# Weighted low powers by exponentials instead of doubling products, modulation rows between the first products, a sine ahead of the arc tangent, one block's seeds three slots earlier

## The chip, the cores and the metric

The kernel runs on one core of a Trainium2 chip. The metric is the device time of one execution in microseconds. The engines are TensorE (PE, with its weight loads PEld), VectorE (DVE), ScalarE (ACT), GpSimd (POOL) and SyncE (SP), which here only issues DMAs. Each engine takes its instructions in program order, and engines wait for each other by semaphores.

## The reference

A layer norm with modulation, a long convolution with a state-space kernel, a residual, a second modulated layer norm, and a bilinear gated unit with a residual. L = 2048 tokens, D = 640 channels, N = 192 states per channel, F = 1536.

```python
sa, ca, ga, sb, cb, gb = (silu(c) @ w_mod).reshape(6, D)
h = layernorm(x) * (1 + ca) + sa
K[d, l] = Re sum_n C[d,n] * exp(dt[d] * A[d,n] * l) * dt[d] * B[d,n]      # l = 0..2047
x = x + ga * (causal_conv(h, K) + h * Dskip)                             # by FFT of length 2 L
h = layernorm(x) * (1 + cb) + sb
x = x + gb * (((h @ w_gate) * (h @ w_up)) @ w_down)
```

## The kernel before

**What is computed where.** The channels are cut into five blocks of 128 (`db`), each into two halves of 64 (`hf`), each half into four groups of 16 channels (`n`, 40 in all). For a group the long kernel K is the product of two small tables over the states: `Pt` holds 32 coarse powers and `Qt` 64 fine powers of each state, each as magnitude times cosine and magnitude times sine. PE multiplies them (`kg`, `kg_ma` and `kg_mb`), ACT copies the result out (`Kt`), and PE runs a four-step FFT of it, the product with the FFT of the input, and the way back (`u_k`, `u_pre`, `u_g`, `u_c`, `u_d`). The FFT work of a block goes on between the tables of later blocks.

**How a group's tables come about.** POOL makes the phases as 32-bit integers (`Ph`, outer sum of low phases `LH` and high phases `DH`), the magnitudes of the coarse table (`EP`, outer product of `LP` and `RH`) and of the fine table (`EQ`, outer product of `LQ` and `RH`): `outer`, L817. ACT takes absolute value, sine and cosine of the phases into a two-buffer ring in PSUM (`tra`, `trb`, function `trig`, three calls a group: `kg_aq`, `kg_ap`, `kg_b`). DVE multiplies them with the magnitudes (`QtA`, `PtA`, `PtB`, `QtB`). `Ph`, `EQ` and `EP` have two buffers each; the `QtA`, `PtB`, `QtB` tiles have one.

**Seeds.** For each block `u_seeds` prepares the state parameters: log radius and frequency (transposed by PE into the layout of the groups), the amplitude `amp` of C times B, and its angle by an arc tangent. Its steps carry letters; `SEG0` (first block) and `SEG` (others) say which steps run in one stretch. Step `r` multiplies the log radii by constants (`RL`, `RH`), step `e` takes exponentials (`LP`, `RH`, `RL`), step `f` makes the argument of the arc tangent, `g` the arc tangent, `h` its transpose, `v` the phase seed `psi`. Each function set of ACT has to be loaded before its functions run: ACT_TABLE_LOAD.

**Low tables.** Once a half, POOL makes `LH` (function `tab_ph`, by additions that double the length) and `LQ` (function `tab_eq`: a copy of the amplitude and three products that double the length: the eight weighted fine powers 0 to 7). Two small POOL operations a half (L752, L753, lambda `weighted`) first put `psi` into the low phases.

**Modulation.** `u_modr` multiplies silu(c) with the columns of `w_mod` for the six modulation rows, on PE in two pieces a row (L458); ACT copies a row out, PE transposes it (`u_fold`, L477), DVE makes the fold `mcol` from them (L481 to L491), which later seeds (`need(1, "gg")`) and the convolution input (`need(1, "sh")`) need. For the first block the gate `ga` is applied by POOL to the convolution's input (L966). `u_stats` takes the layer norm's sums of each of 16 token rows on DVE (L568, L569), `row_stats` makes their scales.

**What sets the order.** A table of numbers, `SCHED`. The program counts slots: group n has three, t = 3n, 3n+1, 3n+2; the number v // 1000 is 2t or 2t+1 and the rest orders the pieces within it. Negative numbers lie in the first block's seeds. Pieces are issued in exactly this order on every engine. A second table, `SLOT`, says which buffer of a ring each use takes. `LATE` holds the exponentials of the second half of the first block, run at slot 15 (`e0`).

After the last group (slot 240) only FFT work remains, then the gated unit, a chain of `fp32r` matrix products on PE with its operands split in high and low parts on ACT, DVE and POOL.

## Time and profile before

| | |
|---|---|
| three runs | 990.01, 992.87, 998.23 us (median 992.87) |
| the profiled execution | 990.33 us, span of its instructions 988.6 us |
| busy in the span | PE 90%, PEld 73%, DVE 77%, ACT 59%, POOL 58% |
| stages by the trace | start and first groups 0 to 100 us; tables and FFT to about 435 us (POOL's last table ends at 435 us); FFT alone to about 490 us; gated unit to the end |

The page gives busy time of each engine, the chain of work that ended last, and groups of equal instructions with busy time, mean duration, and the engine's idle time before them with its releaser. The chain is followed back from the last instruction; an engine that is busy all the time need not be on it. Matmuls are pipelined, so a busy PE is not PE at its peak.

### The profile page before, as it was taken

Reading aid. Unit: us, or ns where it says so; the run is one execution under the profiler, and the core shown is the slowest. Engines: PE = TensorE matmul, PEld = TensorE weight load, DVE = VectorE, ACT = ScalarE, POOL = GpSimd, SP = SyncE. Lnnn points to the kernel's source line nnn. Section 1 sums busy time; section 2 is a strip of 40 time slices with the busy share of each in tenths; the row PEclk is TensorE's granted clock in tenths of the full one; section 3 lists DMA queues with packets and bytes.
Section 4 is the critical chain, followed back from the end, with each engine's and each line's share of the span. In section 5 each row is a group of like instructions: output and inputs, shape, how many; then the busy total and the mean of one; then the engine's idle time right before and its main releaser. Section 6 shows DMA issues by size and latency. Waiting matters only on the chain.

```text
span 988.6 us, 26668 instructions
## 1 busy us (share of the span) xinstructions
PE 887.3 (90%) x11190; PEld 726.3 (73%) x11190; DVE 760.7 (77%) x1311; ACT 579.9 (59%) x1019; POOL 577.4 (58%) x424
## 2 busy tenths in 40 slices
PE   4854898999798699989988999999999999999998
PEld 3643656676575477677666888889998888889998
DVE  8798479887988977896899877787585977677452
ACT  5769999977888797974664322235464332224330
POOL 4987899799779989960145667641022454451000
PEclk9976899999989989999999999999999999999999
DMA  7665666443545553558733453445536222212241
GB/s 243 240 172 196 224 211 205 142 138 120 142 151 142 172 155 106 183 187 281 217 102 106 134 186 104 137 159 168 198 134 216 85 80 80 81 54 77 83 161 54
DMA packets 141961, 148.96 MB, mean 151 GB/s; under 512 B 8976, under 2 KB 120080, under 8 KB 140432
## 3 DMA queue, kind: packets, MB, share of 16 engines
q1 hardware_dynamic: 140688, 146.33, 46.9%
q8 instruction: 88, 1.44, 0.6%
q10 hardware_dynamic: 1152, 0.92, 0.3%
q14 instruction: 33, 0.27, 0.1%
HBM read 108.36 MB, written 38.86 MB: 149 GB/s over the span
## 4 chain that ended last, share of the span: by engine, by line
PE 58%; DVE 14%; ACT 13%; issue 6%; POOL 5%; DMA 2%; SPq 0%; DVEq 0%; ACTq 0%; POOLq 0%
PE pa L1196 26%; PE pa L1611 16%; ACT tra L320 2%; ACT trb L320 2%; PE psfb L995 2%; DVE QtA L872 2%; PE psfc L995 2%; PE psfb L1055 1%; PE kg L928 1%; POOL EQ L817 1%; PE psfa L1055 1%; PE kg L913 1%; PE psfc L1055 1%; PE psfb L950 1%; PE psfa L995 1%
## 5 line engine op out<-in xcount | busy, mean ns | idle before, releaser
L817 POOL TENSOR_TENSOR EQ<-LQ,RH 128x1536 f32<-128x1536 f32 x40 | 124.2, 3105 | 15.1 <-DVE QtB L872 14.9
L320 ACT ACTIVATE z<-pa 128x512 f32<-128x512 f32 x24 | 14.4, 599 | 167.1 <-PE pa L1196 120.5
L1160 DVE TENSOR_TENSOR wsgl<-wga,wsgh 128x640 fp32r<-128x640 f32 x72 | 68.1, 948 | 46.8 <-ACT wsgh L320 46.6
L320 ACT ACTIVATE wsgh<-wga 128x640 fp32r<-128x640 f32 x72 | 52.6, 732 | 72.0 <-PE pa L1611 48.6
L1560 POOL TENSOR_TENSOR z<-z,s 128x512 f32<-128x512 f32 x24 | 33.5, 1394 | 98.6 <-DVE s L1559 98.6
L1611 PE MATMUL pa<-wsgh,sh 128*128 128x384 f32 (+1 forms) x304 | 69.6, 310 | 0.0
L1611 PE MATMUL pa<-wsgh,sl 128*128 128x384 f32 (+1 forms) x304 | 69.2, 308 | 0.0
L1611 PE MATMUL pa<-wsgl,sh 128*128 128x384 f32 (+1 forms) x304 | 69.1, 309 | 0.0
L1172 POOL TENSOR_TENSOR tf<-wur,wgb 128x256 f32<-128x256 f32 x24 | 19.2, 801 | 80.7 <-DVE wtl L1160 54.7
L817 POOL TENSOR_TENSOR EP<-LP,RH 128x768 f32<-128x768 f32 x40 | 66.1, 1652 | 0.0
L817 POOL TENSOR_TENSOR Phb<-LH,DH 128x1536 int32<-128x1536 int32 x20 | 62.3, 3113 | 2.2 <-ACT tra L320 2.1
L817 POOL TENSOR_TENSOR Pha<-LH,DH 128x1536 int32<-128x1536 int32 (+1 forms) x21 | 62.4, 2972 | 1.8 <-ACT trb L320 1.4
L872 DVE TENSOR_TENSOR QtA<-tra,EQ 128x1024 f32<-128x1024 f32 x40 | 47.0, 1216 | 17.0 <-ACT tra L320 8.5
L1160 DVE TENSOR_TENSOR wtl<-tf,wth 128x256 fp32r<-128x256 f32 (+1 forms) x72 | 59.9, 858 | 0.0
L872 DVE TENSOR_TENSOR QtA<-trb,EQ 128x1024 f32<-128x1024 f32 x40 | 47.0, 1215 | 12.2 <-ACT trb L320 7.0
L928 PE MATMUL kg<-QtB,PtB 64*32 64x64 f32 x2560 | 47.0, 225 | 8.1 <-DVE QtB L872 8.0
L928 PEld LDWEIGHTS kg<-QtB,PtB 64*32 64x32 f32 x2560 | 40.3, 112 | 15.5 <-DVE QtB L872 9.0
L1558 DVE TENSOR_TENSOR s<-pa,s 128x512 f32<-128x512 f32 x24 | 16.6, 690 | 45.2 <-PE pa L1196 40.1
L1196 PE MATMUL pa<-sl,wth 128*128 128x512 f32 x144 | 45.2, 395 | 2.1 <-DVE sl L1160 2.1
L1611 PEld LDWEIGHTS pa<-wsgh,sl 128*128 128x128 f32 x304 | 46.6, 188 | 0.0
L1611 PEld LDWEIGHTS pa<-wsgh,sh 128*128 128x128 f32 x304 | 46.5, 188 | 0.0
L1611 PEld LDWEIGHTS pa<-wsgl,sh 128*128 128x128 f32 x304 | 46.5, 188 | 0.0
(602 smaller groups left out, 2926.9 us busy)
## 6 DMA issues: line engine op xcount, KB each, us to landing
wga<-wdg SPq DMA_DIRECT2D x24, 640.0 KB, 3.9
wga<-B_w_gate SPq DMA_DIRECT2D x12, 640.0 KB, 6.1
wgb<-B_w_gate SPq DMA_DIRECT2D x24, 320.0 KB, 3.4
wur<-B_w_up SPq DMA_DIRECT2D x24, 320.0 KB, 3.9
xb<-x2d SPq DMA_DIRECT2D x6, 1280.0 KB, 6.8
TVb<-WD SPq DMA_DIRECT2D x22, 256.0 KB, 3.4
t_tw<-w_mod SPq DMA_DIRECT2D x3, 1600.0 KB, 7.4
t_ti<-w_mod SPq DMA_DIRECT2D x3, 1600.0 KB, 7.5
```

The lines of the kernel that those rows point to most:

```text
L320: return S.activation(o, i, f, **kw)
L817: G.tensor_tensor(o.rearrange("p x (h l) -> p x h l", l=8), lo.unsqueeze(2).to_broadcast([P, rows, nh, 8]), hi.rearrange("p h x -> p x h") ...
L872: return [lambda h=h: V.tensor_tensor(Qt[:, :, :, 32 * h : 32 * h + 32], tr[:, ::-1] if h else tr[:, :, :, ::-1], e[:, :, 32 * h : 32 * h ...
L928: PE.matmul(kg[j * 32 : j * 32 + 32, dd, :], PtB[lo : lo + 64, c, r, :], QtB[lo : lo + 64, c, r, :], start=False, stop=dd == 7 and c == 1, ...
L995: PE.matmul(r[c][par * 64 : par * 64 + 64, i, :], t_tw[:, k0 + k, c, :], src[:, k, :], start=True, stop=True, tile_position=(0, par * 64))
L1055: PE.matmul(r[par][:, i], w, v, start=c == 0, stop=c == 1, tile_position=(lo, 0))
L1160: V.tensor_tensor(lo, v, hi, op=OP.subtract)
L1172: G.tensor_tensor(t[:, 0:2], u[:, 0:2], g[:, 0:2], op=OP.subtract)
L1196: PE.matmul(ps, w[a][:, k], x[b][:, l], start=n == 0 and m == 0, stop=n == 2 and m == len(ks) - 1)
L1558: V.tensor_tensor(S67[i], ps, S6[i], op=OP.add)
L1560: G.tensor_tensor(ZT[i], ZT[i], S67[i], op=OP.add)
L1611: PE.matmul(ACC[tb][t][c], x[:, ts], w[:, cs], start=st, stop=f == NF - 1 and n == 2 and (c == 0 or t % 2 == 1))
```

## The change

1. **Low powers by exponentials.** `tab_eq` with its four POOL operations a half is gone. `LQ` gets three buffers; step `e` now has ACT write the fine powers 1 to 7 as seven exponentials, as it did for `LP`, in place of the exponential of `RL`. DVE weights them with the amplitude, read from PSUM where the transpose put it (new step `q`: a copy and one product). `RL` is now a plain copy of the log radius, and the DVE copies of the amplitude into `RL` are gone. `psi` is added by one POOL operation a block and one a half in place of two a half.
2. **First block.** The exponentials of the second half come with the seeds, directly after the arc tangent, and no longer at slot 15. `EP` of group 1 is made there too.
3. **Modulation rows.** The second and third rows that the fold needs are multiplied between the first products of the groups (slots 6 to 12) instead of ahead of them; the fold moves with them. Loads of later rows follow.
4. **Arc tangent.** In the other blocks a sine of one column (`one_`) stands ahead of the arc tangent, so that the set with the sine is loaded first and the arc tangent finds itself in it.
5. **Seeds.** Of the block `db` = 3 (the third of the four that `u_seeds` prepares during the groups) the last six steps lie three slots earlier; the last two of block 4 one or two.
6. **Smaller ones.** The layer norm's scales are made once for all 16 token rows, not for 6 and 10. The first block's gate is applied by DVE to the convolution's output (`u_d`) instead of by POOL to its input. `trig` without a given absolute value writes it into the cosine's place in the PSUM ring instead of a tile `ab`. Some tiles of the seeds share memory.

```diff
-    mr=(((-87997, 8001), (-87996, 11000)), ((-87999, 2000), (-88997, 8000)), ((-88999, -86998), (-89000, -87998))),
+    mr=(((7000, 11000), (8000, 12000)), ((-87999, 2000), (6000, 9000)), ((-88999, 1100), (-89000, 100))),
...
-        (98000, 116002, 122001, 124001, 126001, 126003, 128000, 129000, 133000, 133001, 134003, 134004, 134005, 134007),
+        (98000, 116002, 122001, 124001, 126001, 126003, 128000, 129000, 130000, 130001, 131500, 131600, 132500, 133500),
...
-SEG0 = ("l", "a", "b", "c", "ud", "r", "x", "e", "f", "G", "g", "D", "h", "v", "R", "")
+SEG0 = ("l", "a", "b", "c", "iud", "r", "x", "e", "f", "Gg", "q", "R", "hv", "DX", "", "Q", "")
...
         def s_e(*hh):
             for l in range(1, 8):
-                act(lp[:, :, :, l], rl[:, :, 0], AF.Exp, scale=64.0 * l)
+                act(lp[:, :, :, l], rl, AF.Exp, scale=64.0 * l)
             act(rh, rh, AF.Exp)
-            act(rl[:, :, 0:3], rl[:, :, 0:3], AF.Exp)
+            for l in range(1, 8):
+                act(lq[:, :, :, l], rl, AF.Exp, scale=float(l))
...
+        def s_q(*hh):
+            lq, a = halves(LQ, hh), T["amp"][:, hh[0] : hh[-1] + 1]
+            V.tensor_copy(lq[:, :, :, 0], a)
+            V.tensor_tensor(lq[:, :, :, 1:8], lq[:, :, :, 1:8], a.unsqueeze(3).to_broadcast([P, len(hh), 96, 7]), op=OP.mult)
...
         def s_g():
             if db:
                 s_G()
+            if db:
+                act(one_, halfpi, AF.Sin)
             act(y, y, AF.Arctan)
...
-    def tab_eq(hf):
-        G.tensor_copy(LQ[:, :, 0:1], rl[:, 3].unsqueeze(2))
-        G.tensor_tensor(LQ[:, :, 1:2], rl[:, 3].unsqueeze(2), rl[:, 0].unsqueeze(2), op=OP.mult)
-        double(LQ, (rl[:, 1], rl[:, 2]), OP.mult)
...
         if ab is None:
-            ab = pk.tile([P, 512], F32, name="ab", bufs=1)
-            av = ab
+            ab = av = cv
...
-        if db == 0:
-            G.tensor_tensor(h, h, xa[:, 4, 0:P].unsqueeze(1).to_broadcast([P, 4, P]), op=OP.mult)
...
+        if db == 0:
+            V.tensor_tensor(ps, ps, ggr.unsqueeze(1).to_broadcast([P, 4, P]), op=OP.mult)
         V.tensor_tensor(xs, ps, xs, op=OP.add)
```

Where the instructions stand. POOL in the first block, before (EP, EQ, Pha and Phb are the tables of the groups; Pha of 768 is half of the first group's):

```order
L817 TENSOR_TENSOR Pha<-LH,DH_155 128x768
L817 TENSOR_TENSOR EP_147<-LP,RH 128x768
L811 COPY LQ<-RL 128x96
L812 TENSOR_TENSOR LQ<-RL 128x96
L777 TENSOR_TENSOR LQ<-LQ,RL 128x96x2
L777 TENSOR_TENSOR LQ<-LQ,RL 128x96x4
L752 TENSOR_TENSOR ptb<-ptb,DL_158 128x96
L753 TENSOR_TENSOR DL_158<-ptb 128x4x24
```

And in the changed kernel, at the same place:

```order
L809 TENSOR_TENSOR Pha<-LH,DH 128x768
L809 TENSOR_TENSOR EP_146<-LP,RH 128x768
L809 TENSOR_TENSOR EP_147<-LP,RH 128x768
L809 TENSOR_TENSOR EQ_144<-LQ,RH 128x1536
L751 TENSOR_TENSOR ptb<-ptb 128x96
L754 TENSOR_TENSOR DL_155<-ptb,DL_155 128x4x24
```

The four LQ operations are gone, and the outer products of EP (group 1) and EQ (group 0) now stand ahead of the phase seed, the two operations on ptb and DL.

ACT in the seeds of the block db = 1, before (the names: LP, RH, RL are the tables of step e, pta the argument of the arc tangent, f16a token rows of the layer norm, trb the trig ring):

```order
L320 ACT_TABLE_LOAD
L320 ACTIVATE LP<-RL 128x2x96 x7
L320 ACTIVATE RH<-RH 128x2x1056
L320 ACTIVATE RL<-RL 128x2x288
L320 ACT_TABLE_LOAD
L320 ACTIVATE pta<-pta 128x192
L320 ACTIVATE f16a<-f16a,nm_97,rs_96 128x640 x2
L320 ACTIVATE PtAa<-Pha 128x1024
L320 ACT_TABLE_LOAD
L320 ACTIVATE trb<-Pha 128x512
```

And now (ptb holds the argument; one__136 is the single column):

```order
L316 ACT_TABLE_LOAD
L316 ACTIVATE LP<-RL 128x2x96 x7
L316 ACTIVATE RH<-RH 128x2x1056
L316 ACTIVATE LQ<-RL 128x2x96 x7
L316 ACT_TABLE_LOAD
L316 ACTIVATE one__136<-halfpi 128x1
L316 ACTIVATE ptb<-ptb 128x192
L316 ACTIVATE f16a<-f16a,nm_94,rs_93 128x640 x2
L316 ACTIVATE PtAa<-Pha 128x1024
L316 ACTIVATE trb<-Pha 128x512
```

Seven exponentials take the place of one, and one load less stands ahead of the next sine. The blocks 2 to 4 get the seven exponentials as well; their number of loads stays.

PE among the first products, before (kg is a group's product, the L458 rows are the modulation rows):

```order
L458 MATMUL psfb<-t_tw,sil 128x256 x5
L458 MATMUL psfa<-t_tw,sil 128x384 x5
L458 MATMUL psfb<-t_ti,sil 128x256 x5
L458 MATMUL psfc<-t_ti,sil 128x384 x5
L458 MATMUL psfa<-t_tw,sil 128x384 x5
L458 MATMUL psfc<-t_tw,sil 128x256 x5
L913 MATMUL kg<-QtA,PtAa 32x64 x32
L928 MATMUL kg<-QtB,PtB 32x64 x32
```

And now:

```order
L456 MATMUL psfb<-t_tw,sil 128x256 x5
L456 MATMUL psfc<-t_tw,sil 128x384 x5
L456 MATMUL psfa<-t_ti,sil 128x384 x5
L906 MATMUL kg<-QtA,PtAa 32x64 x32
L456 MATMUL psfb<-t_ti,sil 128x256 x5
L456 MATMUL psfc<-t_tw,sil 128x384 x5
L921 MATMUL kg<-QtB,PtB 32x64 x32
L456 MATMUL psfa<-t_tw,sil 128x256 x5
L906 MATMUL kg<-QtA,PtAb 32x64 x32
```

Three of the six row pieces now stand behind the first group's first product.

More of the change, by code (lines that the diff above doesn't have):

```diff
@@ L335, in tile_kernel @@
     V.memset(halfpi, math.pi / 2)
-    mults = const.tile([P, 14], F32, name="mults")
-    for k, m in enumerate((1536, 1024, 512, 0, 8, 16, 24, 32, 40, 48, 56, 1, 2, 4)):
+    mults = const.tile([P, 11], F32, name="mults")
+    for k, m in enumerate((1536, 1024, 512, 0, 8, 16, 24, 32, 40, 48, 56)):
         V.memset(mults[:, k : k + 1], float(m))
@@ L577, in u_hm @@
             x = XT[q]
-        need(1, "rs", q < 6)
+        need(1, "rs")
         act(x, x, AF.Identity, scale=rs1[:, q : q + 1], bias=nm1[:, q : q + 1])
@@ L724, in s_G @@
         def s_G():
-            if db:
-                ps = bank("ps2")
-            else:
-                ps = ring(ps_tr, [P, 2, 512], "tr")[:, :, :N]
+            ps = bank("ps2") if db else ring(ps_tr, [P, 2, 512], "tr")[:, :, :N]
             T["ps2"] = ps.rearrange("p c (s r) -> p c s r", r=24)
-            trans(amp, T["ps2"][:, 0])
-            if db == 0:
-                for h in range(2):
-                    act(g4(Rl[h])[:, 3], T["ps2"][:, 0, hs[h]])
+            T["amp"] = ps[:, 0].rearrange("p (h x) -> p h x", h=2)
+            trans(u, T["ps2"][:, 0])
         def s_g():
@@ L1378, in tile_kernel @@
     at(T0["fo"], u_fold)
-    at(T0["e0"], once(lambda: LATE.pop()()))
     for j in range(4):
@@ L1394, in tile_kernel @@
         at(T0["k"][n], u_k, n)
-    for i, f in enumerate((tab_ph, tab_eq)):
-        for hf in range(1, 2 * NB):
-            at(T0["low"][i][hf - 1 : hf], once(f), hf)
+    for hf in range(1, 2 * NB):
+        at(T0["low"][hf - 1 : hf], once(tab_ph), hf)
     man = ctx.enter_context(ExitStack())
```

152 lines of the change are left out of this document (73 added, 79 removed), and 2 rows, old and new, of the table q.

## The prediction

> **What bounds the kernel now.** I read the stages first, by busy time of the engines in three stretches, and the page's row of the chain that ended last. The columns are stretch, length, then busy time (and instructions) of PE, PEld, DVE, ACT, POOL, granted clock, DMA share, GB/s.
>
> ```profile
> 0.00:100.00 100.00, 58.12 (x850) 44.94 (x850) 84.52 (x220) 73.73 (x128) 78.01 (x60) 0.83 0.67 215
> 100.00:435.00 335.00, 294.12 (x6768) 217.89 (x6770) 276.67 (x404) 291.46 (x489) 309.10 (x189) 0.94 0.52 158
> 435.00:545.00 110.00, 98.39 (x1243) 75.72 (x1240) 95.72 (x198) 60.72 (x108) 30.73 (x32) 0.97 0.60 184
> PE 58%; DVE 14%; ACT 13%; issue 6%; POOL 5%; DMA 2%; SPq 0%; DVEq 0%; ACTq 0%; POOLq 0%
> ```
>
> The change touches only what lies before 435 us. From 100 to 435 us POOL is the fullest engine, 309 of 335 us, but PE (294), ACT (291) and DVE (277) are close behind, and POOL has 5% of the chain. A full engine need not be the one that others wait for, so the third view is the waits in that stretch (who waited for whom: us in all, times, longest).
>
> ```profile
> ACT PtAa L320 <- POOL Pha L817: 3.8, 4, 2.5
> DVE QtA L872 <- POOL EQ L817: 2.8, 2, 1.8
> POOL EQ L817 <- DVE QtB L872: 7.1, 2, 4.8
> POOL DL L753 <- issue: 9.5, 2, 8.0
> ```
>
> In 335 us the others wait 3.8 + 2.8 = 6.6 us for tables, while POOL waits 7.1 us for a buffer and 9.5 us for phase seeds, 8.0 of them at one place. So POOL runs ahead with little room, and what paces the stretch is mostly the ring of ACT, DVE and PE.
>
> **What POOL loses.** The groups of the doubling products and of the gate's four multiplications:
>
> ```profile
> L777 POOL TENSOR_TENSOR LQ<-LQ,RL 128x384 f32<-128x384 f32 x10 | 8.8, 881 | 0.8
> L777 POOL TENSOR_TENSOR LQ<-LQ,RL 128x192 f32<-128x192 f32 x10 | 5.6, 559 | 0.8
> L812 POOL TENSOR_TENSOR LQ<-RL 128x96 f32<-128x96 f32 x10 | 4.0, 396 | 0.0
> L811 POOL COPY LQ<-RL 128x96 f32<-128x96 f32 x10 | 3.6, 360 | 2.9 <-DVE RL L747 2.9
> L966 POOL TENSOR_TENSOR hfc<-hfc,f16a 128x512 f32<-128x512 f32 x2 | 2.6, 1297 | 0.0
> L966 POOL TENSOR_TENSOR hfb<-hfb,f16a 128x512 f32<-128x512 f32 x1 | 1.3, 1277 | 0.0
> L966 POOL TENSOR_TENSOR hfa<-hfa,f16a 128x512 f32<-128x512 f32 x1 | 1.3, 1270 | 0.0
> ```
>
> 8.8 + 5.6 + 4.0 + 3.6 = 22.0 us and 2.6 + 1.3 + 1.3 = 5.2 us, together 27.2 us. If POOL paced everything, all of it could come off; if it paced nothing, none. I take the waits that go, **-6.6 us**, since they are what is seen to be paid, and keep 0 and -27.2 as ends.
>
> **The start.** Up to 75 us the trace reads, in order of time (start, length):
>
> ```profile
> 20.92 0.39 POOL L752 TENSOR_TENSOR ptb<-ptb,DL 128x96 int32<-128x96 int32 x1 [1.39 <-DVE ptb L684]
> 30.57 2.31 DVE L872 TENSOR_TENSOR QtA<-trb,EQ 128x1024 f32<-128x1024 f32 x2
> 36.99 3.11 POOL L817 TENSOR_TENSOR Pha<-LH,DH 128x1536 int32<-128x1536 int32 x1
> 47.22 0.17 DVE L481 TENSOR_SCALAR mcol<-psfb 128x5 f32<-128x5 f32 x1 [2.26 <-PE psfb L477]
> 49.74 2.34 DVE L872 TENSOR_TENSOR QtA<-trb,EQ 128x1024 f32<-128x1024 f32 x2
> 72.17 0.17 DVE L371 TENSOR_SCALAR rv<-mv 128x10 f32<-128x10 f32 x1
> 73.77 0.68 DVE L898 TENSOR_TENSOR PtB<-tra,EP 128x512 f32<-128x512 f32 x1
> ```
>
> POOL loses 2.3 us of LQ (one of each kind) and the 1.39 us wait, so its third phase table comes about 3.5 us sooner than 36.99. But the first group's phases then come later, behind two EP and an EQ, and its QtA, which needs their sine, stays near 30.6. DVE fills 84.5 of the first 100 us, so I count its steps. The fold (47.22 to 49.74, 2.5 us) now stands behind the third group's QtA but still waits for the last modulation row, so I take half, -1.3. The second pass of the layer norm's scales (72.17 to 73.77) goes: -1.6. The load of the exponentials' set and the way back (2 x 1.28 us on ACT around 47 and 55 us) become one load in the seeds, where ACT would otherwise idle; ACT then waits for a block's seeds from memory anyway, so nothing more. The weights of the two halves cost DVE some 2 us before 30 us, under POOL's outer products. On SP the loads of two later modulation rows move behind the next block's seed loads; their products keep their slots, far behind, so that is free unless SP is held up for long by the seeds' buffers. **-2.9 us**; the ends are 0 (the rows, now among the products, hold those up) and -5.8 (all of POOL's 3.5 + 2.3).
>
> **ACT.** The rows for its additions (busy us, mean ns, and idle time before with its releaser):
>
> ```profile
> L320 ACT ACT_TABLE_LOAD x23 | 29.5, 1283 | 4.3 <-DMA pta<-A_A_re 4.0
> L320 ACT ACTIVATE LP<-RL 128x192 f32<-128x192 f32 x28 | 10.6, 557 | 0.2 <-DVE RL L690 0.2
> L320 ACT ACTIVATE RL<-RL 128x576 f32<-128x576 f32 x4 | 2.7, 668 | 0.0
> L320 ACT ACTIVATE sil<-ccol 128x5 f32<-128x5 f32 x1 | 0.2, 207 | 0.0
> L320 ACT ACTIVATE ab<-Pha 128x512 f32<-128x512 int32 x22 | 13.8, 625 | 0.1
> L320 ACT ACTIVATE tra<-Phb 128x512 f32<-128x512 int32 x39 | 23.2, 596 | 6.3 <-DVE QtA L872 6.3
> L320 ACT ACTIVATE trb<-Pha 128x512 f32<-128x512 int32 x40 | 23.8, 595 | 3.1 <-DVE QtA L872 2.5 <-DVE PtAb L878 0.4
> 94.33 2.63 ACT LP L320 x7
> 345.30 2.68 ACT LP L320 x7
> ```
>
> The last two are rows of the chain in order of time. Seven fine exponentials are shaped like LP's: 10.6 / 4 = 2.65 us a block, less RL's 0.67, plus 0.2 for the one-column sine (like sil's): +2.2 us a block. Block 1 loses one load, -1.28. In blocks 1 and 4 the LP rows lie on the chain, in 2 and 3 not: 2 x 2.2 - 1.28 = **+3.1 us**. Ends: -1.28 if all hides, +7.5 if all four count.
>
> On the load the Trainium skill (ScalarE: Activation LUTs, What ACT_TABLE_LOAD costs) says that each switch also pays a drain of about 1380 ns, 2.66 us in all. The trace disagrees: of 40 sines that begin a trig call on trb, several right behind a load, the idle time is 3.1 us together, and 2.9 of it is DVE's. By the page the term would be 1.4 us lower.
>
> The absolute value now lands in the trig ring. Before, ACT wrote `ab` while the ring was still held by QtA, and then waited, 6.3 + 2.5 us; now it waits first and the 0.62 us come behind. With waits of 1 to 3 us that is about six times 0.62 = 3.7 us; DVE waits for these sines in part, so half, **+1.8 us** (0 to +3.7).
>
> **DVE.**
>
> ```profile
> L872 DVE TENSOR_TENSOR QtA<-tra,EQ 128x1024 f32<-128x1024 f32 x40 | 47.0, 1216 | 17.0 <-ACT tra L320 8.5 <-POOL LH L799 2.7 <-POOL EQ L817 1.8
> L872 DVE TENSOR_TENSOR QtB<-trb,EQ 128x512 f32<-128x512 f32 x40 | 25.5, 679 | 0.0
> L690 DVE TENSOR_TENSOR RL<-psfa,mults 128x288 f32<-128x288 f32 x6 | 2.7, 444 | 0.0
> 102.27 0.42 DVE L747 COPY RL<-psfa 128x96 f32<-128x96 f32 x2 [3.78 <-PE psfa L629]
> L1110 DVE TENSOR_TENSOR xsa<-psfa,xsa 128x512 f32<-128x512 f32 x3 | 2.0, 679 | 0.0
> ```
>
> A product of 1344 elements isn't in the trace: from 512 (0.68) and 1024 (1.22 us) I extend to 1.55 us, as it too reads one operand from PSUM; ends 1.22 and 2 x 1.22. With a copy of about 0.35 that is 1.9 us a block, less 0.42 (L747) and 2 x 0.2 (RL a copy instead of 0.44): +1.1, four times 4.4; the gate's four products at 0.68 add 2.7. DVE idles 58 of the 335 us and holds 14% of the chain: of 7.1 us I put **+1.0 us** on the path (0 to +7.1). The weighting adds a wait: it needs ACT's last exponential and the transposed amplitude, and behind it in DVE's queue stand `psi` and the next groups' products, so DVE, and POOL for `psi`, wait where ACT is late; that is the second rival below.
>
> **Block 3's seeds.** POOL's 8.0 us stall:
>
> ```profile
> 278.76 0.39 POOL L753 TENSOR_TENSOR DL<-ptb 128x96 int32<-128x96 int32 x1 [8.01 <-issue]
> 289.74 1.06 ACT L320 ACTIVATE PtAa<-Pha 128x1024 f32<-128x1024 int32 x1 [0.32 <-POOL Pha L817]
> ```
>
> Three slot numbers of about 1.7 us (some 400 us for 240) would bring the seed 5 us sooner. Yet ACT waited only 0.32 us for the next phase table: POOL's lead had covered the stall, so I count **0** (already in the 6.6).
>
> **The sum.** -6.6 - 2.9 + 3.1 + 1.8 + 1.0 = -3.6 us on the profiled execution's 990.33, which is 2.5 us under the median of the three runs: **987 us**. After 435 us nothing changes; the last FFT follows in the same order.
>
> **Rivals.** *POOL paces after all.* If its fullness counts and not only the waits seen, the limit moves from POOL to the next engine. POOL worked 309 + 78 = 387 us of 435, so 48 us lie beside it; then ACT, 365 us and about 7.5 more, is the fullest: 373 + 48 = 421, 14 us less: **976 us**. For it: POOL above 90% for hundreds of us with two buffers a table. Against it: the waits, and POOL's 5%.
>
> *The phase seed comes late.* It now stands behind seven more exponentials, the column sine and the weighting on DVE: 2.0 + 0.2 + 1.9 - 0.4 = 3.7 us a block, and behind it on POOL the low phases and the next Ph, for which ACT waits. In block 2 there is no room:
>
> ```profile
> 195.24 3.12 POOL Pha L817
> 198.38 1.06 ACT PtAa L320
> ```
>
> ACT begins 0.02 us behind POOL's table. If that held in all four blocks: 4 x 3.7 - 1.28 - 2.9 = +10.6: **1001 us**. It decides once POOL's lead at the seeds is under 3.7 us. Against it: block 3 swallowed 8 us.
>
> **How the numbers follow.** 0.52 for 987, with an own range of 981 to 993; 0.32 for POOL; 0.16 for the late seed. The range takes in POOL's case and most of the third: 974 to 999. About 1%, 10 us, is what a measurement of this kernel can tell from no change. Faster by more: most of POOL's case and an edge of the first, 0.32. Slower by more: the larger half of the late seeds and dear exponentials, 0.13. The rest, 0.55.
>
> **What would show it.** POOL some 28 us less busy before the tables' end, and that end (435 us) only 3 to 5 us sooner; POOL's idle time grown by about 20 us; ACT some 7 us busier; the LP and LQ rows of blocks 1 and 4 on the chain; the stall at 278 us smaller. I am wrong if the end of the tables moves by over 10 us (POOL paced), or if ACT's waits for Pha grow beyond 10 us (late seeds).

## The result

The changed kernel takes 1040.85 us (median of 4 runs, 1036.28 to 1043.37) against 995.2 us for the kernel before on the same chip: ratio 1.0459, 95% interval 1.0397 to 1.0522, **slower by 46 us**. The forecast was 987 us, with a range from 974 to 999. A few executions reported below (one of noexp at 1265 us, whose trace is therefore not read, one of noweight at 2921 us and one of the kernel before at 2144 us) fell in a much slower state and count in no figure. In the profiled execution (1040.15 us) the tables now end at 484 us, not at 435; the FFT alone and the gated unit behind them take as long as before. The stages of the changed kernel, in the columns of the prediction's first fence:

```profile
0.00:100.00 100.00, 55.76 (x751) 41.35 (x752) 80.11 (x197) 60.05 (x114) 62.02 (x47) 0.81 0.53 178
100.00:484.00 384.00, 308.28 (x6856) 227.92 (x6854) 293.47 (x422) 312.95 (x536) 300.12 (x153) 0.89 0.47 147
484.00:594.00 110.00, 96.72 (x1248) 73.89 (x1249) 96.97 (x199) 61.23 (x109) 30.49 (x31) 1.00 0.60 186
```

Until the tables' end POOL worked 62.02 + 300.12 = 362 us, 25 less than the 387 of before: the work did come off. But its idle time grew from 48 to 484 - 362 = 122 us, and every engine is less full than it was. The waits before 490 us (who waits for whom: us in all, times, longest):

```profile
POOL EQ L809 <- DVE QtB L865: 40.5, 10, 12.2
POOL Pha L809 <- ACT trb L316: 21.8, 9, 5.4
PE kg L906 <- DVE PtAa L871: 15.8, 4, 6.7
POOL ptb L751 <- issue: 15.4, 2, 13.6
PE psfc L1046 <- ACT hfb L316: 11.7, 1, 11.7
```

POOL, said to run ahead "with little room", now waits tens of microseconds for the others to free its buffers. No row of that view has ACT waiting for a phase table any more, and of DVE's waits for POOL 3.3 us are left. So the view shows the 46 us lost at ACT, DVE and PE, and not in waits for POOL's tables. Where they were lost is read from one event that each of the 40 groups has: the start of its first `PtB` product on DVE. Worked out from those starts, in us behind the kernel before (whose time is in the second column); the other columns are experiments told below:

```
group  before   after  late34  start   code  foldps  foldx  codefold  noboth
  0      34.4     5.0     5.1    1.8    2.2     5.5    5.3      1.8     1.8
  2      58.0    10.0     8.2    7.8    7.9     3.3    3.9      3.5     3.8
  5      93.3    14.3    13.8    5.4    5.5     9.0    3.3      1.1     1.3
 11     156.0    19.5    19.4    8.1    8.2    11.1    6.4      3.9     1.7
 15     200.9    24.0    23.7   12.9   13.0    15.6    9.0     10.2     3.0
 21     263.7    24.0    22.9   12.9   12.2    15.5    8.8      9.4     0.8
 22     279.4    38.0    27.3   26.9   16.5    29.5   22.8     13.8     2.7
 29     347.2    41.7    28.9   30.3   17.9    32.7   24.7     15.4     4.6
 30     360.1    47.2    33.1   35.9   22.1    38.3   30.9     19.7     4.9
 39     445.5    50.2    36.0    38.9   25.0    41.3   35.3     22.6     8.1
```

The column "after" is not one loss but several: 14 us in the first 100, 5 more up to group 11, 4.5 up to group 15, 14 at group 22 and 5 at group 30.

### The profile page after: what moved, and what is told of

It reads as the page before. It is cut to its first block, busy times and chain, and to the rows that moved or that the text cites. A ratio compares the mean times of both kernels' runs of the same rounds, so it can differ in the third digit from the quotient of the medians.

```text
span 1038.3 us, 26646 instructions
## 1 busy us (share of the span) xinstructions
PE 898.2 (87%) x11190; PEld 731.6 (70%) x11190; DVE 775.0 (75%) x1307; ACT 588.7 (57%) x1054; POOL 552.0 (53%) x376
## 5 line engine op out<-in xcount | busy, mean ns | idle before, releaser
L809 POOL TENSOR_TENSOR Phb<-LH,DH 128x1536 int32<-128x1536 int32 x20 | 62.2, 3111 | 14.3 <-ACT tra L316 14.3
L865 DVE TENSOR_TENSOR QtA<-tra,EQ 128x1024 f32<-128x1024 f32 x40 | 47.0, 1218 | 14.8 <-ACT tra L316 9.1
L921 PEld LDWEIGHTS kg<-QtB,PtB 64*32 64x32 f32 x2560 | 41.0, 113 | 14.3 <-DVE QtB L865 7.8
```

The lines of the kernel that those rows point to most:

```text
L809: G.tensor_tensor(o.rearrange("p x (h l) -> p x h l", l=8), lo.unsqueeze(2).to_broadcast([P, rows, nh, 8]), hi.rearrange("p h x -> p x h") ...
L865: return [lambda h=h: V.tensor_tensor(Qt[:, :, :, 32 * h : 32 * h + 32], tr[:, ::-1] if h else tr[:, :, :, ::-1], e[:, :, 32 * h : 32 * h ...
L921: PE.matmul(kg[j * 32 : j * 32 + 32, dd, :], PtB[lo : lo + 64, c, r, :], QtB[lo : lo + 64, c, r, :], start=False, stop=dd == 7 and c == 1, ...
```

## Experiments: the order or the operations

The change has new numbers in the table `SCHED` and new operations. Each run's ratio is to the kernel before, run beside it, with a 95% interval in brackets. Three kernels put parts of the table back to the numbers of before.

**late34**: the last six seed steps of block 3 and the last two of block 4.

```diff
-        (98000, ..., 128000, 129000, 130000, 130001, 131500, 131600, 132500, 133500),
-        (134002, ..., 180001, 180003, 182000, 183500),
+        (98000, ..., 128000, 129000, 133000, 133001, 134003, 134004, 134005, 134007),
+        (134002, ..., 180001, 180003, 184000, 184001),
```

> The changed kernel with the slots of block 3's last six seed steps and block 4's last two as before. In the changed kernel's trace the start of the EQ tables falls behind before's by 15 us over block 3's seeds (tables 23 to 25) and 10 us over block 4's (28 to 32). Theory A, the slots: moved ahead, block 3's exponentials stand in front of the copy that PE's inverse transform waits for (11.7 us), and the transposes of the arc tangent in front of transforms that could run; with the old slots 15 to 25 us come back, so about 1016 to 1026 us. Theory B, the operations: the seven more exponentials and the weighting on the vector engine lie on the path of every block wherever they stand; then the slots give back 5 us at most, 1036 to 1041 us.

Measured: 1026.69 us, 1.0322 [1.0266, 1.0378], 1.37% under the changed kernel. A term that the prediction had at 0 costs 14 us; by the table 12.8 of them have come by group 29, behind block 3's seeds, and the rest comes behind block 4's. In the changed kernel, around block 3's seeds (ACT, PE, DVE and POOL, in order of time; in brackets the wait before and its releaser):

```profile
285.16 1.28 ACT L316 ACT_TABLE_LOAD   x1
288.66 2.63 ACT L316 ACTIVATE LP<-RL 128x192 f32<-128x192 f32 x7
292.96 2.60 ACT L316 ACTIVATE LQ<-RL 128x192 f32<-128x192 f32 x7
295.36 0.62 ACT L316 ACTIVATE hfb<-psfc 128x512 f32<-128x512 f32 x1
296.04 0.79 PE L1046 MATMUL psfc<-TVa,t_ti 64*128 64x128 f32 x2 [11.71 <-ACT hfb L316]
302.90 2.35 DVE L865 TENSOR_TENSOR QtA<-trb,EQ 128x1024 f32<-128x1024 f32 x2 [10.07 <-PE kg L906]
307.97 0.59 POOL L751 TENSOR_TENSOR ptb<-ptb 128x192 int32<-128x192 int32 x1 [13.60 <-issue]
```

And in late34:

```profile
284.80 0.59 ACT L316 ACTIVATE hfb<-psfc 128x512 f32<-128x512 f32 x1
285.44 0.49 PE L1046 MATMUL psfc<-TVa,t_ti 64*128 64x128 f32 x2 [1.38 <-ACT hfb L316]
289.24 2.36 DVE L865 TENSOR_TENSOR QtA<-trb,EQ 128x1024 f32<-128x1024 f32 x2 [0.75 <-PE kg L906]
296.55 2.62 ACT L316 ACTIVATE LQ<-RL 128x192 f32<-128x192 f32 x7
305.78 0.59 POOL L751 TENSOR_TENSOR ptb<-ptb 128x192 int32<-128x192 int32 x1 [12.43 <-issue]
```

The steps moved forward (four of the six by three slot numbers, the last two by two and by one) take 10.2 us on ACT in one piece (285.16 to 295.36: two loads, 14 exponentials, `RH`). They now stand ahead of `hfb`, a copy of the FFT of an earlier block that PE waits for. PE waits 11.71 us, the group's product stands behind that FFT step on PE, and DVE waits for the product. With before's slots the copy goes first: PE waits 1.38 us for it, and DVE 0.75 us for the product. The seed itself comes no sooner: the stall that the move was to cover is 13.60 us here and 12.43 with the old slots.

**start**: the slots of the modulation rows, of the row loads on SP, of the fold and of the statistics of six token rows as before.

```diff
-    mr=(((7000, 11000), (8000, 12000)), ((-87999, 2000), (6000, 9000)), ((-88999, 1100), (-89000, 100))),
+    mr=(((-87997, 8001), (-87996, 11000)), ((-87999, 2000), (-88997, 8000)), ((-88999, -86998), (-89000, -87998))),
...
-    fo=(12800, 14500, 18001, 20001),
+    fo=(11001, 12000, 19001, 22000),
```

> The changed kernel with the slots of the modulation rows, the fold, the columns' loads and the statistics as before. The EQ tables of the changed kernel fall 14 us behind between 40 and 90 us. Theory A, the start's order costs them: the fold's short steps now run while POOL computes large tables, and the loads of the later rows stand behind activations that wait; then 10 to 14 us come back, 1027 to 1031 us. Theory B, the first block's new steps (weighting in two halves, one EQ ahead of the phases) cost them and the order of rows and fold is free: under 4 us come back, 1037 to 1041 us.

Measured: 1028.99 us, 1.0359 [1.0304, 1.0414], 1.0% under the changed kernel. At group 5 it is 5.4 us behind, where the changed kernel is 14.3. The row loads on SP come at 40.43 and 51.38 us here, but the fold, told next, still takes 6.9 us (50.90 to 57.84) in place of before's 2.5.

**code**: both sets of numbers put back, so that only the new operations remain.

> The changed kernel's operations (low powers by exponentials and weighting, one-column sine, absolute values in the trig ring, gate on the vector engine, one pass of the scales) with all slots of before. Theory A, the slots cost it all: 985 to 998 us, the prediction's sum without its start. Theory B, the operations cost most: 1020 us or more. If about 10 us remain (998 to 1008), they are block 1's and the late phase seed, 3.7 us a block.

Measured: 1014.76 us, 1.0204 [1.0149, 1.0258], between the ranges of the two theories. So the new order costs 2.5% and the new operations 2.0%. In the table above, order and operations part cleanly: "code" is 5.5 behind at group 5 where the changed kernel is 14.3 behind, and steps up at the seeds of each block.

## Experiments: the fold and POOL

The fold's tiny DVE steps of 128x5 elements run at 0.15 to 0.2 us in the trace of before, with some exceptions that end with a POOL instruction. DVE and POOL, kernel before:

```profile
47.42 0.43 DVE L482 TENSOR_SCALAR mcol<-mcol 128x5 f32<-128x5 f32 x1
49.19 0.48 DVE L489 TENSOR_TENSOR mcol<-mcol 128x1 f32<-128x1 f32 x1
44.72 3.10 POOL L817 TENSOR_TENSOR Phb<-LH,DH 128x1536 int32<-128x1536 int32 x1
49.15 0.54 POOL L799 TENSOR_TENSOR LH<-DL,eighth 128x192 int32<-128x192 int32 x1
```

And the changed kernel, DVE and then POOL:

```profile
53.58 0.11 DVE L479 TENSOR_SCALAR mcol<-psfb 128x5 f32<-128x5 f32 x1
53.93 1.58 DVE L481 TENSOR_TENSOR mcol<-mcol 128x5 f32<-128x5 f32 x1
55.54 3.02 DVE L482 TENSOR_SCALAR mcol<-mcol 128x5 f32<-128x5 f32 x1
58.59 1.56 DVE L483 TENSOR_TENSOR mcol<-mcol 128x5 f32<-128x5 f32 x1
60.19 0.19 DVE L484 RECIPROCAL mcol<-mcol 128x5 f32<-128x5 f32 x1
60.68 2.54 DVE L487 TENSOR_TENSOR dt<-dt,mcol 128x4 f32<-128x4 f32 x1
55.44 3.09 POOL L809 TENSOR_TENSOR EQ<-LQ,RH 128x1536 f32<-128x1536 f32 x1
58.49 1.64 POOL L809 TENSOR_TENSOR EP<-LP,RH 128x768 f32<-128x768 f32 x1
60.09 3.10 POOL L809 TENSOR_TENSOR Pha<-LH,DH 128x1536 int32<-128x1536 int32 x1
```

The step of 3.02 us ends at 58.56, EQ at 58.53; the next at 60.15, EP at 60.13; that of 2.54 at 63.22, Pha at 63.19. Such a step, its operands all in SBUF, waits until POOL's instruction is over, and the trace counts the wait as busy DVE time. RECIPROCAL, which has all in SBUF too, does not wait: it ends at 60.38, while Pha runs. The steps that read PSUM (L479, and L485 and L486 between) do not either. The fold takes 53.58 to 63.28 = 9.7 us instead of 2.5 (47.22 to 49.74).

**foldps**: the changed kernel with the fold's scratch in a PSUM bank, so that no step has two operands in SBUF; one product is added for that.

```diff
...
-        V.tensor_tensor(g1, g1, sg, op=OP.mult)
...
+        gp, gq = (pc[:, 64 + 8 * i : 64 + 8 * i + NB] for i in range(2))
...
+        V.tensor_tensor(gp, gp, sg, op=OP.mult)
...
-        V.tensor_tensor(dt2[:, 1:], dt2[:, 1:], gg[:, 1:], op=OP.mult)
+        V.tensor_tensor(gq, p3[:, 2], g1, op=OP.mult)
+        V.tensor_tensor(dt2[:, 1:], dt2[:, 1:], gq[:, 1:], op=OP.mult)
```

> The changed kernel with the fold's scratch in the bank of PSUM that holds its columns, so that no step has two operands in SBUF or copies SBUF to SBUF, and one product more. In the changed kernel's trace four of the fold's steps, of 0.15 to 0.25 us elsewhere, take 1.58, 3.02, 1.56 and 2.54 us, and each ends within 0.06 us of the end of a POOL instruction. Theory A, a step with operands in SBUF alone has to wait until POOL's running instruction is over: the twelve steps take 2 to 2.5 us together in place of 9.7, PtAa of the third table starts some 7 us sooner, and the time falls by 3 to 7 us (1034 to 1038) since the rows' late loads still hold the place behind. Theory B, they wait for something else that is late there (a semaphore, a write): their durations stay at 9 to 10 us and the time at 1040.

Measured: 1035.99 us, 1.0412 [1.0357, 1.0468], 4.9 us less. The intervals overlap, so the times alone don't show the gain; the trace does. The fold's first step, two more, and the product behind it:

```profile
54.66 0.17 DVE L480 TENSOR_SCALAR psfb<-psfb 128x5 f32<-128x5 f32 x1 [0.53 <-PE psfb L475]
55.27 0.17 DVE L483 TENSOR_SCALAR psfb<-psfb 128x5 f32<-128x5 f32 x1
56.30 0.16 DVE L489 TENSOR_TENSOR dt<-dt,psfb 128x4 f32<-128x4 f32 x1
56.44 1.22 DVE L873 TENSOR_TENSOR PtAa<-tra,EP 128x1024 f32<-128x1024 f32 x1
```

It takes 54.66 to 56.44 = 1.8 us, though POOL works at LH up to 55.95 and at EQ from 55.91 on. The gain at group 2 is 10.0 - 3.3 = 6.7 us, more than the median shows; by group 5 it is 5.3.

**codefold** is code with the same edit.

> The changed kernel's operations at before's slots, with the fold's scratch in PSUM as in the run with the changed kernel. At before's slots the fold took 7.0 us (50.9 to 57.9) against 2.5 in before, four steps again ending with POOL's instructions, and the third group's products are 5.7 us late behind it. Theory A, the waiting for POOL is the whole of the start's loss at these slots: PtB of the fourth group (5.3 us late) is on time within 1 us, and 1009 to 1011 us come in place of 1014.8. Theory B, the first block's new order costs as much by itself: 1013 us or more.

Measured: 1011.11 us, 1.0162 [1.0124, 1.0200], 0.42% under code, again within the noise of the times; at group 5 it is 1.1 us behind, where code is 5.5. There the fold had taken 7.0 us, in the old slots too, since the operations ahead of it put it beside longer POOL instructions.

**before_ab**: the kernel before with only the absolute value written to the trig ring. **before_fold**: with only the fold in PSUM. **before_abfold**: with both.

```diff
...
         if ab is None:
-            ab = pk.tile([P, 512], F32, name="ab", bufs=1)
-            av = ab
+            ab = av = cv
...
```

> The kernel before with one edit: the absolute value of the phases goes into the half of the trig ring that its cosine then overwrites, in place of a tile of its own. Theory A, as predicted: it starts only when the ring is free and puts 0.62 us behind some six waits, half of it on the path, 0 to 4 us: 992 to 997 us. Theory B, it is what makes POOL wait for the phase tables to come free (14.2 + 11.2 us at before's slots, 1.4 + 2.1 before): 8 us or more, 1001 us and above.

> The kernel before with the fold's scratch in PSUM and one product more, nothing else. In before the fold's eleven steps took 2.5 us, since POOL happened to run short instructions there (0.4 to 0.7 us). Theory A, the waiting for POOL is there too but small: the fold takes 1.8 to 2.0 us and the time stays within 2 us of before, 991 to 997. Theory B, the added product and other operands cost or gain something by themselves: more than 3 us off.

> The kernel before with the absolute value in the trig ring and the fold's scratch in PSUM. With the absolute value alone the time rose by 10 us; in its trace the fold starts 3 us later than in before, beside POOL's long tables, and takes 7.4 us in place of 2.5. Theory A, the larger half of that price is the fold's waiting for POOL, which a shift of 3 us brought about: 6 us come back, 997 to 1001 us. Theory B, the absolute value costs 10 us by itself at many groups and the start is made up for later: 1003 us or more.

Measured: before_ab 1006.06 us, 1.0101 [1.0053, 1.0149]; before_fold 992.52 us, 0.9978 [0.9950, 1.0007]; before_abfold 999.52 us, 1.0029 [0.9998, 1.0060]. The absolute value alone costs 0.5%, some 5 us, and in before_ab twice as much. The rest came through the fold. In before_ab it starts some 3 us later than before, beside EQ, and four of its steps are held (0.81, 1.42, 2.51 and 1.61 us). The longest of them (DVE, then POOL):

```profile
53.61 2.51 DVE L489 TENSOR_TENSOR mcol<-mcol 128x1 f32<-128x1 f32 x1
53.02 3.08 POOL L817 TENSOR_TENSOR EQ<-LQ,RH 128x1536 f32<-128x1536 f32 x1
```

That is why the fold in PSUM gains nothing that can be seen by itself in the kernel before (its interval holds 1) and 0.4 to 0.7% in the others: what a held step costs depends on which POOL instruction it meets. In late34, whose start has the changed kernel's order, the fold begins 4 us later, two steps are held for 0.88 and 1.56 us, and it takes 3.9 us.

## Experiment: the queue of SP

In the changed kernel SP's queue from 53 to 70 us (SPq rows are DMA issues), and who waited for the loads:

```profile
53.85 0.37 SPq L557 DMA_DIRECT2D ghc<-A_u  x1
67.92 0.33 SPq L557 DMA_DIRECT2D gha<-A_u  x1
68.82 0.38 SPq L449 DMA_DIRECT2D t_ti<-w_mod  x1
69.30 0.47 SPq L449 DMA_DIRECT2D t_tw<-w_mod  x1
67.00 0.89 DVE L565 BATCH_NORM_STATS2 st<-gha 128x6 f32<-128x320 f32 x2
77.17 5.96 PE L456 MATMUL psfc<-t_ti,sil 128*128 128x384 f32 x10 [6.12 <-DMA t_ti<-w_mod]
81.96 0.89 DVE L565 BATCH_NORM_STATS2 st<-Wb 128x6 f32<-128x320 f32 x2 [6.51 <-DMA Wb<-A_u]
```

The load of token rows into `gha` can only be issued when DVE has taken the statistics of the rows there, at 67.89. Behind it in the same queue stand the two modulation rows. They need nothing but their own free tiles, and wait from 53.85 to 68.82, 15 us (in foldps, where the statistics come sooner, to 62.06); then PE waits 6.12 us for them, and DVE 6.51 us for the token rows behind them.

**foldx**: foldps with the three token-row loads moved behind the two row loads on SP; nothing else.

```diff
-        (5001, 22003),
+        (8503, 22003),
...
-        (1000, 20000),
-        (1, 19000),
+        (8502, 20000),
+        (8501, 19000),
```

> The changed kernel with the fold's scratch in PSUM and three of the activations' loads (for the statistics of three row groups) put behind the loads of the two later modulation rows on SP's queue. With the fold alone in PSUM the first products of the sixth group are still 9.0 us late, against 5.3 at before's slots with the slow fold. Theory A, those 9 us come from the rows' loads, issued at 68.8 and 69.3 us behind loads that wait for the statistics, 1.6 MB each, ahead of the load for which the vector engine waits: with the rows first 3 to 6 us come back, 1030 to 1033 us. Theory B, the rows wait for PE's reading of the tables' space and not for the queue: within 2 us of the run with the fold alone, 1034 to 1038 us.

Measured: 1026.10 us, 1.0319 [1.0281, 1.0356], 0.93% under foldps. The same rows, now:

```profile
54.15 0.38 SPq L449 DMA_DIRECT2D t_ti<-w_mod  x1
64.90 3.49 PE L456 MATMUL psfc<-t_ti,sil 128*128 128x384 f32 x10
70.28 0.87 DVE L567 BATCH_NORM_STATS2 st<-Wb 128x6 f32<-128x320 f32 x2
```

PE and DVE wait for neither load, and the product takes 3.49 us for 5.96. The profiled executions show 6 us of the gain at the tables' end (41.3 to 35.3), the medians 9.9; the spread of the runs doesn't settle which is nearer. The run start, whose row loads came earlier and whose fold was still held, had given back 1.0%, near the 0.93% of the queue alone.

## Experiments: the new operations

All of these start from codefold (old order, fold in PSUM), 1.62% behind the kernel before. **noexp** is codefold without the seven fine exponentials in the blocks 1 to 4 (the tables then hold no true powers), **noweight** without the product that weights them, **noboth** without either.

```diff
-            for l in range(1, 8):
+            for l in range(1, 8) if db == 0 else ():
                 act(lq[:, :, :, l], rl, AF.Exp, scale=float(l))
```

> The operations at before's slots with the fold in PSUM (1011.1 us), but in blocks 1 to 4 the seven exponentials of the fine powers are left out, so that the EQ tables there hold no true powers; the weighting still runs. They are 7 x 0.28 = 2.0 us of ACT a block, ahead of the next group's sine. Theory A, they lie on the path in all four blocks: 8 us less, 1001 to 1005 us. Theory B, as in the prediction in two of four: 4 us less, 1006 to 1008 us. Theory C, the weighting alone holds the seeds: under 2 us, 1009 to 1013 us.

> The same base, but in blocks 1 to 4 the product that weights the powers (1.55 us on the vector engine ahead of the phase seed) is left out, so that only the power 0 is weighted. Theory A, all of it lies on the path: 4 x 1.55 = 6 us less, 1003 to 1007 us. Theory B, as in the prediction a seventh to a quarter: 1 to 2 us less, 1009 to 1012 us.

> The same base with both left out in blocks 1 to 4: no fine exponentials, no weighting product (the EQ tables hold no true powers). What is left against before is the absolute value in the ring (3 us), the one-column sine, the gate on the vector engine and the start. Theory A, both lie on the path one behind the other: 12 to 14 us less, 996 to 1000 us. Theory B, one hides the other: the same as the better of the two alone. If it stays above 1004 us, another of the new operations costs as much.

Measured: noexp 999.16 us, 1.0047 [1.0016, 1.0078]; noweight 1010.18 us, 1.0145 [1.0077, 1.0213]; noboth 998.19 us, 1.0031 [1.0003, 1.0058]. The weighting is worth 0.17%, nothing that can be told from 0. The exponentials are worth 1.15%, 11.4 us, with some 5 us of uncertainty either way. What was taken away is the whole work of one group of ACT (the rows are the changed kernel's; the second is the weighting):

```profile
L316 ACT ACTIVATE LQ<-RL 128x192 f32<-128x192 f32 x28 | 10.6, 557 | 0.0
L714 DVE TENSOR_TENSOR LQ<-LQ,psfc 128x1344 f32<-128x1344 f32 x3 | 4.6, 1549 | 0.0
```

So the measured gain fits all 10.6 us lying on the path, and the table shows that all four blocks pay. From codefold to noboth (there without the weighting too) the two part by 2.2 us at group 11, 7.2 at 15, 11.1 at 22 and 14.8 at 30. DVE's waits show two ways. Behind block 4's seeds it waits for sines, which stand behind the exponentials on ACT. The product `QtA` there, in codefold and in noboth:

```profile
372.07 2.36 DVE L867 TENSOR_TENSOR QtA<-trb,EQ 128x1024 f32<-128x1024 f32 x2 [4.32 <-ACT trb L316]
```

```profile
358.78 2.36 DVE L869 TENSOR_TENSOR QtA<-trb,EQ 128x1024 f32<-128x1024 f32 x2 [1.83 <-ACT trb L316]
```

DVE's wait for the sines is 2.49 us longer with the exponentials, and they take 10.6 / 4 = 2.65 us a block. In block 1 DVE waits in the seeds themselves: step `q`'s copy of the amplitude heads its queue and waits for PE's transposes, the last of which stands behind the exponentials and the arc tangent. Again codefold, then noboth:

```profile
105.39 0.51 DVE L715 COPY LQ<-psfa 128x192 f32<-128x192 f32 x1 [5.84 <-PE psfa L628]
```

```profile
103.09 0.53 DVE L716 COPY LQ<-psfa 128x192 f32<-128x192 f32 x1 [3.29 <-PE psfa L629]
```

That is 2.55 us more; in block 3 the same wait is 4.56 us against 1.60. In block 2 it is `PtAb` that waits for sines, 3.67 us against 0.4.

noboth also measures what POOL's saved work brought. It still has POOL without its `LQ` products. Busy times in the columns of the first fence, noboth and then before_abfold:

```profile
100.00:440.00 340.00, 294.87 (x6740) 218.93 (x6744) 274.89 (x399) 288.96 (x485) 288.02 (x149) 0.93 0.50 156
```

```profile
100.00:441.00 341.00, 296.88 (x6724) 219.75 (x6727) 273.59 (x399) 291.82 (x485) 309.00 (x189) 0.93 0.51 156
```

POOL works 21 us less in the same stretch, and the times are 1.0031 and 1.0029. So POOL's less work and the smaller edits that the two have unlike come to nothing together; which of them gives and which takes isn't shown.

Two kernels moved the weighting. **weightlate** puts it behind the phase seed in a slot of its own (37000, 87000, 135000, 185000); **psi1** converts the phase seed ahead of it.

> As the run of the operations at before's slots with the fold in PSUM, but in blocks 1 to 4 the weighting of the low powers (0.5 + 1.55 us on the vector engine) stands behind the phase seed and behind the next group's product instead of ahead of both. Theory A, of the 2.6 to 5 us that a block loses, two are the exponentials (2.0 on ACT ahead of the next sine) and the rest is the weighting that holds up the phase seed, PtA and PE: 4 blocks give back 1 to 2 us each, 1002 to 1007 us. Theory B, ACT alone paces the seeds: nothing comes back, 1009 to 1011 us.

> The same base with nothing left out, but the phase seed's conversion on the vector engine stands ahead of the weighting (2.06 us) in place of behind it. Theory A, POOL's chain of low phases waits for it and the others for POOL: up to 2 us a block, 1003 to 1008 us. Theory B, PtA behind the weighting is what matters, which stays where it is: 1009 to 1012 us.

Measured: weightlate 1018.02 us, 1.0237 [1.0200, 1.0274], slower; psi1 1011.28 us, 1.0167 [1.0115, 1.0220], no change. That the weighting makes the phase seed late is not where time goes. weightlate gained some 3 to 5 us on codefold in block 2 and lost about 5 in each of blocks 1 and 4; the amplitude then holds its PSUM bank longer, which may be why, but was not tried.

**codeabpt** writes the absolute value of the third trig call into the `PtB` tile in place of the ring.

```diff
...
-        tr = trig(PH[n].rearrange("p (a r) m -> p a (r m)", a=2)[:, :, 512:768])
+        tr = trig(PH[n].rearrange("p (a r) m -> p a (r m)", a=2)[:, :, 512:768], None, PtB.rearrange("p c r m -> p (c r m)"))
```

> The changed kernel's operations at before's slots, fold in PSUM, and the absolute value of the third part of a group in the tile that its product fills afterwards (free by then), not in the trig ring. What is left against before is the exponentials in place of POOL's products, the weighting, the one-column sine, the gate on the vector engine and the single pass of the scales. Theory A, exponentials and weighting cost 2 to 3 us a block: 1000 to 1006 us. Theory B, the ring's absolute value was the cause of the late seeds too: 996 us or less. Theory C, it adds nothing once the fold is mended: 1009 to 1012 us.

Measured: 1015.25 us, 1.0194 [1.0130, 1.0258]: not faster, against the hope that a place off the ring would do. `PtB` has one buffer, and ACT now waits 16.8 us, in ten places, for PE to be done with it: the same wait with another name.

**lppool**: the kernel before with the fold in PSUM, and POOL making four of the seven powers of `LP` in blocks 1 to 4, so that ACT has 1.5 us a block less (4/7 of 2.65).

> The kernel before with the fold in PSUM (992.5 us against 994.5 of before) and the change's trade the other way round: in blocks 1 to 4 ACT computes three of the seven coarse exponentials (powers 1, 2 and 4) and POOL makes the other four by two products a half block (96 and 288 elements). ACT loses 4 x 0.38 = 1.5 us a block, POOL gains about 1.1 us a half block. Theory A, ACT is what all wait for at every block's seeds and POOL has room: 4 to 6 us less than with the fold alone, 987 to 990 us. Theory B, ACT was at the edge only, and without the added exponentials it has room: no difference, 991 to 995 us. Theory C, POOL's added products stand in front of the tables: slower, 996 us or more.

Measured: 995.74 us, 1.0020 [0.9999, 1.0042] against 0.9978 for before_fold: no gain, rather a loss of 0.4%. Less ACT work than before buys nothing where POOL takes it over; whether ACT had room there, or POOL's products cost what ACT's gave, this run can't part.

**mended**: foldx with late34's slots and with codeabpt's edit.

> The changed kernel with everything mended that the runs so far name: fold in PSUM, the three loads behind the modulation rows', the seeds of blocks 3 and 4 at before's slots, the absolute value out of the trig ring. Only the start's order of rows and fold and the new operations are left of the change. Theory A, the causes add up: 1026 less 14 to 16 for the seeds' slots and 6 to 9 for the ring, 1001 to 1006 us, no faster than the operations at before's slots with the same mending. Theory B, they hide one another: 1010 us or more. Theory C, the start's order is a gain once its two faults are gone: under 999 us.

Measured: 1017.20 us, 1.0221 [1.0158, 1.0283], above the 1001 to 1006 us of theory A, which had the ring at 6 to 9 us. From the single effects: 1.0319 - 0.0137 + 0.0032 = 1.0214. So within the intervals the causes add, and the new order of the start, freed of its two faults, shows no gain over the old one (codeabpt, 1.0194). None of the kernels beats the kernel before by more than is uncertain.

The whole, each step by the two ratios it lies between:

| cause | per cent | from |
|---|---|---|
| seeds of blocks 3 and 4 earlier | 1.37 | after, late34 |
| seven exponentials in each of four blocks | 1.15 | codefold, noexp |
| row loads behind token rows on SP | 0.93 | foldps, foldx |
| fold held by POOL | 0.47 | after, foldps |
| absolute value in the ring | 0.3 to 0.5 | before_fold, before_abfold; noboth |
| weighting | 0 to 0.2 | codefold, noweight; noexp, noboth |
| together | 4.2 to 4.6 | of 4.59 |

Each of these differences is uncertain by 0.4 to 0.8, so that the sum comes out this well is in part luck. By the times alone the fold's and the weighting's can't be told from 0.

## Why the prediction was wrong

**What bounds the kernel.** Right as far as it went: "what paces the stretch is mostly the ring of ACT, DVE and PE". From it, though, the POOL term should have been 0. The -6.6 us were waits for POOL; they went (ACT's 3.8 us to none), and noboth against before_abfold shows no net gain from 21 us less POOL work. The waits for POOL were even more than the prediction read: the same view has DVE waiting 2.7 and 2.4 us for LH and 1.1 for EP. That such a wait turns into one for the next engine of the ring fits this, but isn't shown by itself.

**The start, -2.9 us.** The sign was wrong, by two steps. "Its products keep their slots, far behind, so that is free unless SP is held up for long by the seeds' buffers" named the queue but not its blocker: the token-row loads, which wait for statistics on DVE, 0.93%. And the fold, "I take half, -1.3", was priced as 2.5 us of DVE work; it became 9.7 us beside POOL's long tables, 0.47%. The rows of before that show the hold, 0.43 and 0.48 us among steps of 0.15, had not been laid beside POOL's.

**ACT, +3.1 us.** "In blocks 1 and 4 the LP rows lie on the chain, in 2 and 3 not" failed: all four blocks paid. By noexp the exponentials cost 11.4 us; less four times 0.67 for RL's, plus four times 0.2 for the column sine, less the load of 1.28, that is 8.2 us, just beyond the far end of the range given (+7.5), with the 5 us of uncertainty of noexp; the other three terms were not tried by themselves. That ACT was not on the old kernel's chain in blocks 2 and 3 did not mean that it had 2 us to spare there.

**The absolute value, +1.8 us (0 to 3.7).** Mis-sized: 3 to 5 us by itself. In before_ab it also pushes the fold under EQ, another 5 to 7; no step of the prediction joined these two.

**DVE, +1.0 us.** Right as far as the runs can tell: the product takes 1.549 us (forecast 1.55), and without it 0.17%, 2 us, is gained, within the noise. The gate's products and the copies were not tried by themselves.

**Block 3's seeds, 0.** Here the step asked only whether POOL's stall was covered. It was; but the six steps are queued on ACT, PE and DVE too, and there they were put ahead of an FFT copy that PE waits for: 14 us with block 4's two steps, the largest single cause.

**The rivals.** *POOL paces* is refuted: 25 us off POOL, and its idle time grew by 74. *The phase seed comes late* came near in price: four times 3.7 = 14.8 us for the exponentials and the weighting, and 1011.11 - 998.19 = 12.9 us from codefold to noboth. Its way is half the one seen. As it said, DVE waits at the weighting for the seed in blocks 1 and 3; in 2 and 4 it waits for sines in ACT's own queue. The wait of ACT for POOL's phases, whose growth beyond 10 us was its sign, vanished, and converting the phase seed ahead of the weighting changed nothing. POOL does wait longer for the seeds, 31 us in codefold and 17 in noboth; whether any of that is paid is open. No rival had a price for the reordering of block 3 or of SP's queue.

**The signs given.** POOL 25 us less busy (28 said), ACT 373 us for 365 (7 more said): right. The tables' end came 49 us later, not 3 to 5 us sooner; POOL's idle by 74, not 20; the stall at 278 us became 13.6 us, not smaller. The chain's LP and LQ rows can't be judged: the chain of this execution goes back along PE only through the FFT and the gated unit.

## What to carry to other kernels

Moving a step in a hand-written order moves it on every in-order queue it issues to: list, for each engine and for the DMA queue, which instruction it now stands ahead of and who waits for that one. Where three engines pace a ring with little slack, work taken off the fourth can be worth nothing, as POOL's 21 us here. Work put on one of the three may cost its full length in every block, as the exponentials on ACT did, or nothing that can be seen, as the weighting on DVE; the chain of the old execution does not tell which. A short step that takes several times its usual duration and ends with another engine's instruction is a wait counted as work; before moving it, look at what it would then lie beside.

## What the runs showed of the hardware

**DVE waits for POOL's instruction.** Steps of 1 to 5 elements a partition took 1.56 to 3.02 us in place of 0.15 to 0.2, each ending within 0.05 us of POOL's instruction; with one operand in PSUM they did not (1.8 us in place of 9.7 for the fold). RECIPROCAL, SBUF to SBUF, took 0.19 us while POOL was at Pha. The Trainium skill (SBUF — State Buffer, SBUF: two separate sides) says that DVE and GpSimd share a pair of ports as an exclusive lock for the whole instruction, which a DVE operation takes with two SBUF inputs or in a two-port mode. The trace agrees, with the numbers above. Whether the held steps with a single input (L482, 3.02 us) ran in a two-port mode, no run here shows.

**An idle PE comes back slow.** After the 12 us wait of block 3 in the changed kernel (columns as in the first fence; the granted clock stands third from the end):

```profile
284.00:296.00 12.00, 0.33 (x24) 0.17 (x12) 8.25 (x14) 11.72 (x23) 7.80 (x3) 0.63 0.15 52
296.00:300.00 4.00, 3.96 (x32) 3.96 (x32) 0.00 (x0) 3.94 (x7) 0.00 (x0) 0.50 0.48 131
```

The first 4 us after it run at a granted clock of 0.50, and the FFT's matmuls of 64x128 that read 0.27 us at full clock (315 us) read 0.42 and start 0.21 us apart in place of 0.11, two at a time. In late34 the same matmuls come after a wait of only 1.38 us, at a granted clock of 1.00 and 0.27 us each. So a long wait on PE can cost more than its length: here, by an estimate from the spacing, about 2 us on top of 11.71.
